# A fused attention and two-stage expert kernel: one normalization moved, two queues of small work re-placed, one output group reordered

## The chip, the cores and the metric
The kernel runs on one core of one Trainium2 chip. The metric is the device time of one execution in microseconds (us), as the median of several runs. One further execution was recorded by the hardware profiler, and all rows of the trace come from that one.

## What is computed
Three steps run one after the other; the second takes the first one's rows (2304 tokens of 512 values), the third takes the second one's.

```python
scores = scale * q @ k.T ; scores += min(-(cum_i - cum_j), 0)   # causal
attn = exp(scores - max); attn /= sum; x = attn @ v             # 4 x 8 heads, 576 x 64
...
e = argmax(x @ w_gate); gate_w = softmax(x @ w_gate)[e]         # 8 experts
x = gate_w * (relu(x @ w1[e]) @ w2[e])                          # 512 -> 1024 -> 512
...
xn = x / sqrt(mean(x*x) + 1e-6) * rms_g
out = (silu(xn @ w_gate2) * (xn @ w_val)) @ w_out               # 512 -> 1536 -> 512
```

## The kernel before, in words
All matrix products are in float32 split into two parts, high and low: a value is rounded by one engine (the high part, a cast) and the remainder is formed by another (the low part, a subtraction). A product is three matmuls, high by high, high by low and low by high.

**Attention** (to about 212 us of the trace) works on 16 pairs of heads. Its last part routes the tokens: `route` (L404 to L483) is a generator that computes the expert of each token, scatters the rows into one region of memory per expert with five indirect DMAs of GpSimd, and then calls `order_experts` (L486 to L537). That function sorts the experts by their count and writes the small table `nb`: where each expert's piece begins, who it is, and flags that are read at the very end. All of it is tiny VectorE instructions. A list `RANK` says how many steps of this generator are put behind each of the eight first products of expert 0.

**The experts** (`moe`, L857 to L952). Expert 0 is done first, in two portions: its first 256 rows ("early rows", in memory already), and 128 "late rows", which arrive with the last scatter and are loaded as `xl`. `gemm1` makes eight blocks of the hidden layer; each block ends with a Relu on ScalarE (L770) and a VectorE subtraction (L771). `gemm2` (L783) makes four column blocks. The late rows go through `rows_gemm1` (L821), are turned around by TensorE in `turn_tile` (L749, then the cast L751 on ScalarE and the subtraction L752 on VectorE), and go through `rows_gemm2` (L832). `finish` (L802) normalizes a portion's rows: a matmul that sums squares (L805), a square root on ScalarE (L807), a reciprocal (L808) and four multiplications (L811) on VectorE; `keep` (L795) sends the result to memory. `scaled_rows` and `turn_rows` (L849) do the same for the late rows. `x_transpose` (L738, L741, L742) prepares the rows of expert 1. In between, `split` takes the next piece of the experts' weights from its staging buffer, with a cast on ScalarE (L650) and a subtraction on GpSimd (L651), and then starts the load of another piece on SyncE's queue. Four staging buffers exist.

**The last stage** (`glu`, from about 460 us) has six groups of 384 tokens. Its first half (`glu_gemm1`, L1061) is one long run of matmuls. Its second half multiplies by the output weights: 72 steps n, each for one group g and one block f of twelve. A step's left operand was split six steps ahead by `glu_split` (cast L1076 on ScalarE, subtraction L1077 on GpSimd) and its nine matmuls are in `glu_gemm2` (L1086). Steps 0 to 23 alternate between the groups 0 and 1. The output weights arrive as 64-bit floats and are rebuilt by `decode`: bit operations and comparisons on VectorE (L1004, L1006, L1010, L1012, L1014), an absolute value on ScalarE (L1008), a rounding copy on VectorE (L1016, the cast) and a subtraction on GpSimd (L1017). Twelve such pieces are decoded ahead of the steps 1, 3, 5, 7, 9 and 11, two at each; four buffers hold them while they are rebuilt. At f = 11 a group's three tiles of outputs are copied by ScalarE (L1089) and scattered by an indirect DMA of GpSimd (L1090).

**The order of the work.** TensorE, ScalarE and VectorE run the instructions in the order of the program text; SyncE's queue too, inside `moe`. GpSimd's order, and SyncE's elsewhere, is chosen when the program is built, by data dependences. So an instruction that waits holds up all that is behind it on its engine.

Of the kernel before, what the change touches and what calls it, by code (L numbers as in the profile page):

```python
# [7 lines left out]
F32 = mybir.dt.float32  # L8
# [9 lines left out]
NTOK = B * S  # L18
# [4 lines left out]
NA = 256  # L23
# [618 lines left out]
def split(k, n=1, pool=None, bufs=0):  # L642
    nc = k.nc
    for _ in range(n):
        if k.staged:
            s, u, q, raw = k.staged.pop(0)
            if q == 0:
                new_unit(k, s, u)
            w = k.wt[s, u][:, q:q + 2]
            nc.scalar.copy(w[:, :, 0, :], raw)  # L650
            nc.gpsimd.tensor_tensor(w[:, :, 1, :], raw, w[:, :, 0, :].bitcast(F32), op=ALU.subtract)  # L651
            if pool or k.spool:
                feed(k, pool or k.spool, bufs or STG)
# [71 lines left out]
def x_transpose(k, s, kcs, tiles):  # L725
    if s not in k.xq:
        k.xq[s] = [k.rpool.tile([128, 4, CM], F32R, name=f"xt{n}{s}", tag=f"xt{n}", bufs=1) for n in range(2)]
    turn(k, k.x[s], tiles, k.xq[s], kcs)
# [16 lines left out]
def turn_tile(k, x, hi, lo):  # L745
    nc = k.nc
    ps = k.psum.tile([128, 512], F32, name=f"xq{k.uid()}", tag="b")
    for c in range(4):
        nc.tensor.transpose(ps[:, 128 * c:128 * c + 128], x[:, 128 * c:128 * c + 128], k.ident)  # L749
    p3 = ps.rearrange("p (c n) -> p c n", c=4)  # L750
    nc.scalar.copy(hi, p3)  # L751
    nc.vector.tensor_tensor(lo, p3, hi.bitcast(F32), op=ALU.subtract)  # L752
# [41 lines left out]
def keep(k, y, n, column):  # L794
    k.nc.sync.dma_start(out=k.ytd[:, :, bass.ds(column, n)], in_=y)  # L795


def column(k, piece):
    return number(k, OFF + piece, NTOK)


def finish(k, s, n):  # L802
    nc = k.nc
    ps = k.psum.tile([128, 512], F32, name=f"ms{s}", tag="b")
    nc.tensor.matmul(ps[:, 0:n], k.ones32, k.sq[s][:, 0:n], start=True, stop=True)  # L805
    r = k.sq[s][:, 0:n]
    nc.scalar.activation(r, ps[:, 0:n], AF.Sqrt, bias=k.eps6, scale=1.0 / DM)  # L807
    nc.vector.reciprocal(r, r)  # L808
    y = k.y[s][:, :, 0:n]
    for c in range(4):  # L810
        nc.vector.scalar_tensor_tensor(y[:, c, :], y[:, c, :], k.gv[:, c:c + 1], r, op0=ALU.mult, op1=ALU.mult)  # L811
    return y
# [44 lines left out]
def moe(k, close):  # L857
    k.y, k.sq = {}, {}

    def rank(n):  # L860
        for _ in range(n):
            next(k.last, None)

    spool, k.spool = k.spool, None
    feed(k, spool, STG, 2)
    k.order = [(s, u, q) for s in range(1, E) for u in range(4) for q in (0, 2)]
    row = ids(k, k.x[0], EARLY)
    keep_ids(k, row, 0)
    rank(RANK[0])
    for f in range(8):  # L870
        gemm1(k, 0, f, NA)
        rank(RANK[f + 1])
        if f == 3:
            load_late(k)
            load_x(k, 1)
            k.spool = spool
            feed(k, k.spool, STG, STG)
        if f < 2:
            split(k)
    first = tiles_of(CAP[0])  # L880
    gemm2(k, 0, 0, NA)
    gate(k, k.xl, ((0, 128),))
    gemm2(k, 0, 1, NA)
    xb = [k.rpool.tile([128, 4, CM], F32R, name=f"xb{n}", tag=f"xt{n}", bufs=1)[:, :, 0:128] for n in range(2)]
    turn_tile(k, k.xl[:, 0, :], *xb)
    row = ids(k, k.xl, ((0, 128),))
    keep_ids(k, row, column(k, 1))
    split(k)
    gemm2(k, 0, 2, NA)
    gate(k, k.x[1], first)  # L890
    split(k)
    gemm2(k, 0, 3, NA)
    split(k)
    k.hr = y_tile(k, "hr")[:, 0:1024]
    rows_gemm1(k, xb, 0)
    split(k)
    rows_gemm1(k, xb, 1)
    y = finish(k, 0, NA)
    hb = [k.mpool.tile([128, 8, CM], F32R, name=f"hb{n}", tag=f"h{n}")[:, :, 0:128] for n in range(2)]
    turn_tile(k, k.hr[:, 0:512], *[t[:, 0:4] for t in hb])  # L900
    x_transpose(k, 1, (0, 1), first)
    turn_tile(k, k.hr[:, 512:1024], *[t[:, 4:8] for t in hb])
    split(k)
    x_transpose(k, 1, (2, 3), first)
    row = ids(k, k.x[1], first)
    keep(k, y, NA, 0)
    yr = y_tile(k, "yr")[:, 0:1024].rearrange("p (a n) -> p a n", a=2)
    k.yr = yr[:, 0, :]
    rows_gemm2(k, hb)
    keep_ids(k, row, column(k, 2))  # L910
    split(k)
    for s in range(1, E):
        last = s == E - 1
        head = iter(())
        n = CAP[s - 1]
        if last:
            close()
            head = glu_head(k)
            next(head)
        else:  # L920
            load_x(k, s + 1)
        for f in range(8):
            gemm1(k, s, f, n)
            if s == 1 and f == 0:
                y = yr[:, 1, :].rearrange("p (c n) -> p c n", c=4)
                turn_rows(k, k.yr, y)
            if s > 1 and f == 1:
                y = finish(k, s - 1, CAP[s - 2])
            if f == 5:
                keep(k, y, CAP[s - 2] if s > 1 else LATE, column(k, s))  # L930
                if not last:
                    gate(k, k.x[s + 1], tiles_of(CAP[s]))
            if f % 2 or (s == 1 and f < 4):
                split(k)
            next(head, None)
        for c in range(4):
            gemm2(k, s, c, n)
            if not last:
                if c in (1, 2):
                    x_transpose(k, s + 1, (2 * c - 2, 2 * c - 1), tiles_of(CAP[s]))  # L940
                if c == 1:
                    row = ids(k, k.x[s + 1], tiles_of(CAP[s]))
                if c == 3:
                    keep_ids(k, row, column(k, s + 2))
            split(k)
            next(head, None)
    assert not k.staged and not k.order

    def tail():
        keep(k, finish(k, E - 1, CAP[-1]), CAP[-1], column(k, E))  # L950

    k.tail = tail  # L952


RANK = (9, 0, 17, 10, 0, 0, 0, 0, 0)


def glu_tiles(k, pool, tag, shape, n, dt=F32):
# [38 lines left out]
    nc.vector.tensor_tensor(high, high, low, op=ALU.bitwise_or)  # L997


def decode(k, loads):  # L1000
    nc = k.nc
    both = [(raw[:, :, 0], raw[:, :, 1], raw.bitcast(F32)[:, :, 1], w) for raw, w in loads]
    for low, high, hf, w in both:
        nc.vector.tensor_scalar(low, low, 29, None, op0=ALU.logical_shift_right)  # L1004
    for low, high, hf, w in both:
        nc.vector.scalar_tensor_tensor(low, high, 0xC0000000, low, op0=ALU.bitwise_and, op1=ALU.bitwise_or)  # L1006
    for low, high, hf, w in both:
        nc.scalar.activation(hf, hf, AF.Abs)  # L1008
    for low, high, hf, w in both:
        nc.vector.tensor_scalar(hf, hf, TINY, None, op0=ALU.max)  # L1010
    for low, high, hf, w in both:
        nc.vector.tensor_scalar(high, high, 3, 0x3FFFFFFF, op0=ALU.logical_shift_left, op1=ALU.bitwise_and)  # L1012
    for low, high, hf, w in both:
        nc.vector.tensor_tensor(high, high, low, op=ALU.bitwise_or)  # L1014
    for low, high, hf, w in both:
        nc.vector.tensor_copy(w[:, 0, :], hf)  # L1016
        nc.gpsimd.tensor_tensor(w[:, 1, :], hf, w[:, 0, :].bitcast(F32), op=ALU.subtract)  # L1017


# [57 lines left out]
    nc.gpsimd.tensor_tensor(c[:, 1, :], h, c[:, 0, :].bitcast(F32), op=ALU.subtract)  # L1077


def glu_gemm2(k, acc, n):  # L1080
    g, f = k.seq[n]
    w, c = k.wo[f], k.ring[n % 12]
    for t in range(3):
        cols = slice(128 * t, 128 * t + 128)
        for i, (a, b) in enumerate(((0, 0), (0, 1), (1, 0))):
            k.nc.tensor.matmul(acc[g][t], c[:, a, cols], w[:, b, :], start=f == 0 and i == 0, stop=f == 11 and i == 2)  # L1086
        if f == 11:
            o = new_raw(k).bitcast(F32).rearrange("p d two -> p (d two)")
            k.nc.scalar.copy(o, acc[g][t])  # L1089
            i = k.nc.gpsimd.indirect_dma_start(  # L1090
                out=k.out, out_offset=bass.IndirectOffsetOnAxis(ap=k.oid[:, g, t:t + 1], axis=0),
                in_=o, in_offset=None, bounds_check=NTOK - 1, oob_is_err=False,
            )
            of_rows(k, k.outs, i.ins, ())


def glu_head(k):
# [19 lines left out]
def glu(k):  # L1117
# [67 lines left out]
    for n, (g, f) in enumerate(k.seq):  # L1185
        if f == 0:
            acc[g] = [k.psum.tile([128, 512], F32, name=f"go{k.uid()}", tag="b") for _ in range(3)]
        if n < 24 and g == 1 and f + 6 < NF:
            decode(k, weights[0:2])
            weights = weights[2:]  # L1190
            if f + 8 < NF:
                weights += load_out(k, f + 8)
        if n + ahead < len(k.seq):
            glu_split(k, n + ahead)
        glu_gemm2(k, acc, n)
# [185 lines left out]
```

## Time and profile before

| what | value |
|---|---|
| median of 3 runs | 929.44 us (929.34 to 929.82) |
| the profiled execution, its own time | 934.07 us |
| its span, first to last instruction | 932.3 us |
| TensorE (matmuls) busy | 889.3 us, 95% |
| VectorE, ScalarE, GpSimd busy | 460.2, 410.8, 332.9 us |
| share of TensorE in the chain of work that ended last | 84% |
| share of VectorE in that chain | 6% |

The profiled execution took 4.6 us longer than the median, and its time holds 1.8 us outside the span. In a row of the timeline the first two numbers are the start and the length in us; xN counts merged instructions; what stands in brackets is the idle time of the engine just before and what ended it. In a row of windows each engine has its busy time and a count, then follow TensorE's granted clock (1.00 is full speed), the share of the DMA engines and the rate.

### The profile page before, as it was taken

To read this page: it belongs to the slowest core of one execution; us is meant where nothing else is said; L and a number is where in the kernel's file an instruction comes from. 1 tells how busy PE (TensorE), PEld (TensorE's weight loads), DVE (VectorE), ACT (ScalarE), POOL (GpSimd) and SP (SyncE) were. 2 spreads that over 40 slices of the span, in tenths; PEclk is the share of its full clock that TensorE was granted. 3 is DMA by queue.
4 is the path that set the end of the run, shared out by engine and by line. 5 is a ranking of instruction groups with operands and counts; after the bars stand their busy time and mean duration, and the time that the engine had idled before them with its cause. 6 is when DMAs were issued, how large, how long until landed. Compare 5 with 4: busy or idle time off the path is not lost.

```text
span 932.3 us, 15830 instructions
## 1 busy us (share of the span) xinstructions
PE 889.3 (95%) x5684; PEld 781.1 (84%) x5684; DVE 460.2 (49%) x1339; ACT 410.8 (44%) x1009; POOL 332.9 (36%) x320
## 2 busy tenths in 40 slices
PE   6999999998799999999899999999999998899995
PEld 3666666668699999999899999999999995588884
DVE  4555664637524354544685555444554699700000
ACT  5887887873655566665531111111111122333310
POOL 2001321034566667676111110011100146797541
PEclk9999999999999999999999999999999999999998
DMA  7996686323646566666531101111011122110001
GB/s 236 291 295 193 180 233 183 97 97 90 227 154 194 174 193 195 196 182 210 166 102 46 46 26 43 46 46 45 27 43 46 46 100 81 47 68 35 35 34 37
DMA packets 51388, 111.59 MB, mean 120 GB/s; under 512 B 6064, under 2 KB 14027, under 8 KB 51299
## 3 DMA queue, kind: packets, MB, share of 16 engines
q1 hardware_dynamic: 48339, 100.95, 35.7%
q0 software_dynamic: 2912, 9.46, 2.7%
q8 instruction: 47, 0.77, 0.3%
q14 instruction: 42, 0.34, 0.1%
q10 hardware_dynamic: 48, 0.07, 0.0%
HBM read 89.69 MB, written 20.76 MB: 118 GB/s over the span
## 4 chain that ended last, share of the span: by engine, by line
PE 84%; DVE 6%; issue 4%; POOL 3%; ACT 2%; DMA 1%; POOLq 0%; DVEq 0%; ACTq 0%
PE gg L1061 32%; PE g L783 11%; PE g L767 8%; PE go L1086 8%; PE t L306 6%; PE pvy L352 5%; PE s L261 5%; PE tl L380 3%; PE sm L274 2%; DVE raw L1014 1%; DVE raw L1004 1%; PE xp L738 1%; PE r L832 1%; POOL gx5b L1077 1%; PE r L821 1%
## 5 line engine op out<-in xcount | busy, mean ns | idle before, releaser
L1061 PE MATMUL gg<-gx,ws 128*128 128x384 f32 x1728 | 300.4, 335 | 0.0
L1061 PEld LDWEIGHTS gg<-gx,ws 128*128 128x128 f32 x1728 | 299.6, 188 | 0.1
L651 POOL TENSOR_TENSOR u<-raw,u 128x1024 fp32r<-128x1024 f32 x64 | 154.3, 2422 | 104.4 <-ACT u L650 100.4
L1017 POOL TENSOR_TENSOR ws<-raw,ws 128x256 fp32r<-128x256 f32 x48 | 36.7, 786 | 259.2 <-DVE ws L1016 259.2
L783 PE MATMUL g<-h,u 128*128 128x256 f32 (+7 forms) x768 | 109.0, 301 | 5.4 <-DVE h L771 4.2
L783 PEld LDWEIGHTS g<-h,u 128*128 128x128 f32 x768 | 104.5, 194 | 6.5 <-DVE h L771 4.6
L767 PE MATMUL g<-xt,u 128*128 128x256 f32 (+7 forms) x768 | 104.2, 295 | 0.0
L1067 ACT ACTIVATE gh<-gg 128x384 f32<-128x384 f32 x72 | 35.3, 491 | 152.9 <-PE gg L1061 152.9
L767 PEld LDWEIGHTS g<-xt,u 128*128 128x128 f32 x768 | 101.4, 188 | 0.8
L1008 ACT ACTIVATE raw<-raw 128x256 f32<-128x256 f32 x72 | 28.1, 442 | 124.9 <-DVE raw L1006 112.4
L287 ACT ACTIVATE p<-sc,nm 128x128 f32<-128x128 f32 (+3 forms) x128 | 72.4, 572 | 12.0 <-DVE nm L247 8.3
L1068 DVE TENSOR_TENSOR gh<-gg,gh 128x384 f32<-128x384 f32 x72 | 40.0, 555 | 74.8 <-ACT gh L1067 74.8
L247 DVE CUSTOM_DVE_ANT_0 sc<-s,in 128x128 f32<-128x128 f32 (+3 forms) x128 | 57.5, 489 | 39.0 <-PE s L264 19.9
L650 ACT CAST u<-raw 128x1024 fp32r<-128x1024 f32 x64 | 67.2, 1050 | 4.0 <-DMA raw<-in_w 4.0
L339 ACT COPY pt<-t 128x512 f32<-128x512 f32 (+3 forms) x160 | 62.2, 433 | 11.6 <-PE t L306 7.4
L306 PE MATMUL t<-ident,p 128*128 128x128 f32 x400 | 62.2, 281 | 1.6 <-ACT p L287 1.5
L1069 DVE TENSOR_TENSOR gh<-gg,gh 128x384 f32<-128x384 f32 x72 | 40.2, 558 | 44.8 <-PE gg L1061 41.6
L791 DVE TENSOR_TENSOR sq<-sq,sn 128x256 f32<-128x256 f32 (+7 forms) x24 | 15.7, 653 | 87.8 <-ACT sn L790 87.8
L352 PE MATMUL pvy<-pt,vp 128*64 128x512 f32 (+4 forms) x320 | 50.8, 433 | 1.5 <-ACT pt L339 0.8
L261 PE MATMUL s<-in 64*128 64x128 f32 (+3 forms) x256 | 51.5, 491 | 0.0
L306 PEld LDWEIGHTS t<-ident,p 128*128 128x128 f32 x400 | 43.8, 141 | 6.9 <-ACT p L287 2.2
L234 POOL COPY in<-in 64x64 f32<-64x64 f32 x32 | 8.0, 251 | 116.0 <-DMA in<-in_q 106.0
(232 smaller groups left out, 1207.4 us busy)
## 6 DMA issues: line engine op xcount, KB each, us to landing
raw<-in_w SPq DMA_DIRECT2D x64, 512.0 KB, 4.3
in<-cumd SPq DMA_DIRECT2D x30, 256.0 KB, 5.1
xs<-zrow SPq DMA_DIRECT2D x8, 771.0 KB, 10.2
raw<-in_wg SPq DMA_DIRECT2D x24, 256.0 KB
raw<-in_wv SPq DMA_DIRECT2D x24, 256.0 KB, 3.0
raw<-in_wo SPq DMA_DIRECT2D x24, 256.0 KB, 2.6
vp<-in_v SPq DMA_DIRECT2D x16, 320.0 KB, 5.9
in<-in_q SPq DMA_DIRECT2D x16, 288.0 KB, 5.3
```

The costliest lines, as they stand in the source:

```text
L247: k.nc.vector.tensor_tensor_reduce(out=out, in0=ps, in1=bias, scale=-0.125, scalar=3e38, op0=ALU.add, op1=ALU.min, accum_out=accum)
L261: nc.tensor.matmul(ps[h], st.q[r, 128 * i:128 * i + 128], st.k[r, 0:w], start=True, stop=False)
L287: k.nc.scalar.activation(out, st.s[i, h][:, 0:w], AF.Exp, bias=st.nm[:, n:n + 1], scale=-1.0, accum_out=acc)
L306: nc.tensor.transpose(ps[:, off:off + 128], src[:, 128 * j:128 * j + 128], k.ident)
L339: nc.scalar.copy(b, a)
L352: nc.tensor.matmul(st.y[r, a - 64:512], st.v[:, h, j, :], k.pt[:, h, o:o + S - a], start=j == 0, stop=j == 4)
L650: nc.scalar.copy(w[:, :, 0, :], raw)
L651: nc.gpsimd.tensor_tensor(w[:, :, 1, :], raw, w[:, :, 0, :].bitcast(F32), op=ALU.subtract)
L767: nc.tensor.matmul(ps[:, 0:n], w[:, f % 4, a, 128 * kc:128 * kc + 128], x[b][:, kc, 0:n], start=kc == 0 and i == 0, stop=kc == 3 and i == 2)
L783: nc.tensor.matmul(ps[:, 0:n], w[:, f % 4, a, 128 * c:128 * c + 128], k.h[b][:, f, 0:n], start=f == 0 and i == 0, stop=f == 7 and i == 2)
L1061: nc.tensor.matmul(ps, w[:, m, a, 128 * kc:128 * kc + 128], b[:, kc, :], start=kc == 0 and n == 0, stop=kc == 3 and n == 2)
L1086: k.nc.tensor.matmul(acc[g][t], c[:, a, cols], w[:, b, :], start=f == 0 and i == 0, stop=f == 11 and i == 2)
```

## The change
Four edits, none of which changes what is computed.

1. In `moe`, `finish(k, 0, NA)` moves behind both turned halves of the late rows, both transposes of expert 1 and one `split`; that `split` stays behind the transposes, which are no longer parted by it. The DMA `keep(k, y, NA, 0)` moves behind `rows_gemm2`. The late rows' result is written over `hr`, not into a new tile.
2. `RANK` spreads the end of the generator: three steps instead of ten behind the third product, then 1, 1, 1, 2, 2.
3. The rounding copy of the output weights, in the twelve pieces that are decoded between the steps, goes from VectorE to ScalarE.
4. In the last four steps (group 5, f from 8 to 11) the matmuls run tile by tile, each tile through its four blocks, so two tiles of outputs are complete before the third one's matmuls begin; the third tile's copy is shared by ScalarE and VectorE, half each.

```diff
@@ moe
     rows_gemm1(k, xb, 1)
-    y = finish(k, 0, NA)
     hb = [k.mpool.tile([128, 8, CM], F32R, name=f"hb{n}", tag=f"h{n}")[:, :, 0:128] for n in range(2)]
     turn_tile(k, k.hr[:, 0:512], *[t[:, 0:4] for t in hb])
     x_transpose(k, 1, (0, 1), first)
     turn_tile(k, k.hr[:, 512:1024], *[t[:, 4:8] for t in hb])
+    x_transpose(k, 1, (2, 3), first)
     split(k)
-    x_transpose(k, 1, (2, 3), first)
+    y = finish(k, 0, NA)
     row = ids(k, k.x[1], first)
-    keep(k, y, NA, 0)
-    yr = y_tile(k, "yr")[:, 0:1024].rearrange("p (a n) -> p a n", a=2)
+    yr = k.hr.rearrange("p (a n) -> p a n", a=2)
     k.yr = yr[:, 0, :]
     rows_gemm2(k, hb)
+    keep(k, y, NA, 0)
     keep_ids(k, row, column(k, 2))
...
-RANK = (9, 0, 17, 10, 0, 0, 0, 0, 0)
+RANK = (9, 0, 17, 3, 1, 1, 1, 2, 2)
@@ decode
-        nc.vector.tensor_copy(w[:, 0, :], hf)
+        (cast or nc.vector.tensor_copy)(w[:, 0, :], hf)
@@ glu_gemm2
+def glu_part(k, acc, n, t):
...
+        if g == NG - 1 and t == 2:
+            k.nc.scalar.copy(o[:, 0:256], acc[g][t][:, 0:256])
+            k.nc.vector.tensor_copy(o[:, 256:512], acc[g][t][:, 256:512])
+        else:
             k.nc.scalar.copy(o, acc[g][t])
...
+LASTF = 4
...
+    if n < len(k.seq) - LASTF:
+        for t in range(3):
+            glu_part(k, acc, n, t)
+    elif n == len(k.seq) - 1:
+        for t in range(3):
+            for m in range(LASTF):
+                glu_part(k, acc, n + 1 - LASTF + m, t)
@@ glu
-            decode(k, weights[0:2])
+            decode(k, weights[0:2], k.nc.scalar.copy)
```

## Rows read from the trace of the kernel before

**Rows 1.** Timeline of TensorE's matmuls, expert 0 and the late rows.
```profile
227.84 6.27 PE L783 MATMUL g<-h,u 128*128 128x256 f32 x38 [2.67 <-DVE h L771]
...
233.95 0.60 PE L749 MATMUL xq<-ident,xl 128*128 128x128 f32 x4
...
240.14 5.74 PE L821 MATMUL r<-u,xb 128*128 128x512 f32 x24
...
249.11 0.50 PE L832 MATMUL r<-u,hb 128*128 128x512 f32 x1
254.60 7.42 PE L832 MATMUL r<-u,hb 128*128 128x512 f32 x23 [4.99 <-DVE hb L752]
```

**Rows 2.** Timeline of VectorE, the same stretch.
```profile
224.72 0.15 DVE L516 CAST nb<-ogot 1x7 uint32<-1x7 f32 x1
...
226.91 1.73 DVE L771 SCALAR_TENSOR_TENSOR h<-g,h 128x256 fp32r<-128x256 f32 x5
...
248.34 1.75 DVE L808 RECIPROCAL sq<-sq 128x256 f32<-128x256 f32 x1 [3.00 <-ACT sq L807]
250.13 3.82 DVE L811 SCALAR_TENSOR_TENSOR y<-y,gv,sq 128x256 f32<-128x256 f32 x4
253.87 0.68 DVE L752 TENSOR_TENSOR hb<-xq,hb 128x512 fp32r<-128x512 f32 x1
```

**Rows 3.** Granted clock and busy time, four microseconds inside `rows_gemm2`.
```profile
254.00:258.00 4.00, 3.40 (x8) 2.72 (x9) 2.70 (x6) 0.00 (x0) 0.00 (x0) 0.50 0.79 250
```

**Rows 4.** Timeline of ScalarE, expert 0 and the late rows.
```profile
232.42 0.72 ACT L722 ACTIVATE xl<-xl 128x512 f32<-128x512 f32 x1 [0.56 <-DMA xl<-xs]
...
245.92 0.60 ACT L823 ACTIVATE hr<-r 128x512 f32<-128x512 f32 x1 [0.46 <-PE r L821]
246.53 1.28 ACT L807 ACT_TABLE_LOAD   x1
```

**Rows 5.** Line 811 over the whole trace: count, shortest, median and longest ns.
```profile
L811 DVE SCALAR_TENSOR_TENSOR y<-y,gv,sq x32: 471/520/2754, 250.1 to 466.8; 128x256 f32<-128x256 f32 x4, 128x312 f32<-128x312 f32 x4, 128x304 f32<-128x304 f32 x4, 128x300 f32<-128x300 f32 x4
```

**Rows 6.** Timeline of GpSimd, one weight subtraction in that stretch.
```profile
250.93 2.34 POOL L651 TENSOR_TENSOR u<-raw,u 128x1024 fp32r<-128x1024 f32 x1 [1.01 <-ACT u L650]
```

**Rows 7.** Timeline of VectorE, the decoding of output weights.
```profile
753.54 0.76 DVE L1014 TENSOR_TENSOR raw<-raw 128x256 uint32<-128x256 uint32 x2
...
777.06 2.38 DVE L1014 TENSOR_TENSOR raw<-raw 128x256 uint32<-128x256 uint32 x2
...
779.77 1.60 DVE L1004 TENSOR_SCALAR raw<-raw 128x256 uint32<-128x256 uint32 x2
...
785.52 0.49 DVE L1016 CAST gx2b<-raw 128x256 fp32r<-128x256 f32 x2
...
807.87 2.40 DVE L1014 TENSOR_TENSOR raw<-raw 128x256 uint32<-128x256 uint32 x2
```

**Rows 8.** Timeline of GpSimd, the same stretch.
```profile
776.88 2.28 POOL L1077 TENSOR_TENSOR gx5b<-gh,gx5b 128x384 fp32r<-128x384 f32 x2 [1.81 <-ACT gx5b L1076]
779.73 1.50 POOL L1017 TENSOR_TENSOR gx2b<-raw,gx2b 128x256 fp32r<-128x256 f32 x2 [0.57 <-DVE gx2b L1016]
```

**Rows 9.** Timeline of ScalarE, the same stretch.
```profile
781.79 0.78 ACT L1008 ACTIVATE raw<-raw 128x256 f32<-128x256 f32 x2 [4.58 <-DVE raw L1006]
```

**Rows 10.** Timeline of TensorE, its last wait in the output products.
```profile
808.87 1.88 PE L1086 MATMUL go<-gx3b,gx4b 128*128 128x512 f32 x7 [0.48 <-POOL gx4b L1077]
```

**Rows 11.** DMA issues by tile: count, size, median us from issue to landing.
```profile
raw<-in_wo SPq DMA_DIRECT2D x24, 256.0 KB, 2.6
```

**Rows 12.** Timeline of ScalarE, the last outputs.
```profile
920.55 0.59 ACT L1089 COPY raw<-go 128x512 f32<-128x512 f32 x1 [20.17 <-PE go L1086]
921.29 1.29 ACT L1089 COPY raw<-go 128x512 f32<-128x512 f32 x2 [0.16 <-PE go L1086]
```

**Rows 13.** Timeline of GpSimd, the last outputs.
```profile
921.41 0.99 POOL L1090 DMA_INDIRECT out<-raw,oid  x1 [15.18 <-ACT raw L1089]
...
923.99 0.98 POOL L1090 DMA_INDIRECT out<-raw,oid  x1 [0.30 <-issue]
```

More of the change, by code (lines that the diff above doesn't have):

```diff
@@ L997, in as_f32, with decode @@
     nc.vector.tensor_tensor(high, high, low, op=ALU.bitwise_or)
-def decode(k, loads):
+def decode(k, loads, cast=None):
     nc = k.nc
@@ L1077, in glu_split, with glu_gemm2 @@
     nc.gpsimd.tensor_tensor(c[:, 1, :], h, c[:, 0, :].bitcast(F32), op=ALU.subtract)
-def glu_gemm2(k, acc, n):
+def glu_part(k, acc, n, t):
     g, f = k.seq[n]
     w, c = k.wo[f], k.ring[n % 12]
[L1083 to L1088, printed above, removed]
-            k.nc.scalar.copy(o, acc[g][t])
[L1090 to L1094, printed above, removed]
+    cols = slice(128 * t, 128 * t + 128)
+    for i, (a, b) in enumerate(((0, 0), (0, 1), (1, 0))):
+        k.nc.tensor.matmul(acc[g][t], c[:, a, cols], w[:, b, :], start=f == 0 and i == 0, stop=f == 11 and i == 2)
+    if f == 11:
+        o = new_raw(k).bitcast(F32).rearrange("p d two -> p (d two)")
+        if g == NG - 1 and t == 2:
+            k.nc.scalar.copy(o[:, 0:256], acc[g][t][:, 0:256])
+            k.nc.vector.tensor_copy(o[:, 256:512], acc[g][t][:, 256:512])
+        else:
+            k.nc.scalar.copy(o, acc[g][t])
+        i = k.nc.gpsimd.indirect_dma_start(
+            out=k.out, out_offset=bass.IndirectOffsetOnAxis(ap=k.oid[:, g, t:t + 1], axis=0),
+            in_=o, in_offset=None, bounds_check=NTOK - 1, oob_is_err=False,
+        )
+        of_rows(k, k.outs, i.ins, ())
+LASTF = 4
+def glu_gemm2(k, acc, n):
+    if n < len(k.seq) - LASTF:
[5 more added lines that the diff above has]
+                glu_part(k, acc, n + 1 - LASTF + m, t)
 def glu_head(k):
```

## The prediction, made before the changed kernel ran

> **What bounds the kernel now.** I read the page first: TensorE is busy for almost the whole span and holds most of the chain of waits, so time can only come from TensorE's gaps and its slow stretches. Then the timeline of TensorE, looking in brackets for what ended each gap, and the other engines' timelines at those places. Four places touch the change.
>
> *Expert 0's second product.* TensorE has started `gemm2` and then stands 2.67 us [rows 1] for a low part of the hidden layer: VectorE makes the last five only after the whole expert ordering, from 226.91 us [rows 2].
>
> *The late rows.* The first matmul of `rows_gemm2` runs at 249.11 us; then TensorE stands 4.99 us for `hb` [rows 1]. VectorE was busy with the early rows' normalization, a reciprocal of 1.75 and multiplications of 3.82, and made the first `hb` at 253.87 [rows 2]. After the gap the clock is at half speed, 0.50, the 1.2 GHz level [rows 3]: 23 matmuls take 7.42 us where 24 of the same width in `rows_gemm1` took 5.74 [rows 1].
>
> *The output weights.* Six decodings, from 777.06 to 807.87 us, follow each other in a loop of (807.87 - 777.06) / 5 = 6.16 us [rows 7]. The two steps that each feeds need 18 matmuls; nine of this width take about 2.1 us (the 7 at 808.87 take 1.88 [rows 10]), so TensorE needs some 4.1 us of a loop and waits the rest. Its last such wait ends at 808.87, on GpSimd's low part [rows 10].
>
> *The end.* The third copy of outputs ends at 921.29 + 1.29 = 922.58 [rows 12]; its indirect DMA begins at 923.99 because GpSimd is still issuing the one before [rows 13].
>
> **The change part by part.** The sums are made in the profiled execution, 934.07 us, which is 4.6 us or 0.5% above the median of 929.44; I subtract the same gain from the median.
>
> *Ordering spread.* Nothing is added or removed; the same VectorE instructions stand elsewhere. The fourth low part can now start at about 224.8, behind the step that writes `nb` at 224.72 [rows 2], the last ones around 227.6 to 228.4, each one delayed by the small steps still ahead of it. So the column block ends some 2 us earlier at best. But the next thing on TensorE, the turn of the late rows at 233.95 [rows 1], needs rows that land and are scaled until 232.42 + 0.72 = 233.14 [rows 4]. That load waits for the scatters, which the change leaves alone. What is late next is thus the late rows, and the gain is 233.95 - 233.2 = **0.75 us**; the bounds are 0, if the clock falls all the same and stays low longer, and 0.8. I take 0.75, as either clock reaches 233.2. ScalarE keeps up: it stood 0.46 us before the late Relu [rows 4], and TensorE's second turn needs that Relu only after the first turn and a transpose.
>
> *Normalization behind the splits.* The four turned blocks go first on VectorE. Their subtractions read PSUM and need about 0.68 each [rows 2], ScalarE's casts about as much as the Relu of the same size, 0.60 [rows 4]. So both `hb` are there when TensorE, which has the same transposes to do as now, comes to `rows_gemm2` where its first matmul already stands: 249.11 [rows 1]. It then ends at 249.11 + 5.74 = 254.85 in place of 254.60 + 7.42 = 262.02: **7.17 us**, of it 4.99 the gap and 2.2 the slow clock. The cost is hidden: the square root comes behind the five casts, the split and the table load of 1.28 [rows 4], at about 251; reciprocal 1.75 [rows 2]; four multiplications at the median of 0.52 [rows 5], to about 254.8. The late rows need VectorE's next reciprocal at about 255 (matmuls to 254.1 with the lead of 0.75, then two ScalarE passes). The cover is thin. If it fails, TensorE waits at the transposes of `yr`. In `keep` one DMA moves on SyncE's queue; behind it stand the ids and the next weight load, and that load waits anyway for a buffer that the next split frees, so nothing is late. The tile saved costs nothing. Bounds: 4.99 (the clock stays low) to 7.9.
>
> *Casts on ScalarE.* Per decoding VectorE loses two copies of together 0.49 [rows 7]; ScalarE gains two, which I price like its Abs passes on the same buffers, 0.78 for two [rows 9]. But more moves than that. On ScalarE the splits of the left operands now stand behind these casts, which wait for L1014. So GpSimd's four subtractions come in one run, weights first. Now the L1014 pair takes 2.38 while GpSimd subtracts (776.88 to 779.16 [rows 8]) and 0.76 when alone [rows 7]; L1004 likewise shares 1.60 with GpSimd's 1.50 [rows 7, 8]. In the rows a VectorE instruction and a GpSimd one alternate, at 0.75 per pair for the weights (1.50 / 2) and 1.14 for the splits (2.28 / 2). The new loop, from the start of L1014: 0.4 for its first half, 0.4 cast, 0.15 handover; then 1.50 + 2.28 of GpSimd with L1004, L1006 and half of L1010 between; then some 0.7 of L1010 and L1012, an estimate as two fifths of the loop's rest (6.16 - 2.38 - 0.49 - 1.60 = 1.7). Sum 5.4 us, over five loops 5 x 0.73 = 3.6 saved. Against it, the operand that TensorE waits for last: now it comes 808.87 - 807.87 = 1.0 after L1014 began [rows 7, 10], then 0.95 + 1.50 + 1.0 = 3.4 after: 2.4 lost. Net **1.2 us** gained. Bounds: below, the case of full blocking (a rival); above, a loop of 4.7, at which the reload of a buffer (2.6 [rows 11], after 0.95 + 1.50) becomes the bound: 5 x 1.46 - 2.4 = 4.9.
>
> The Trainium skill (SBUF — State Buffer, "Who interferes with whom") says that a VectorE instruction with two SBUF inputs and a GpSimd one that reads SBUF exclude each other for the whole instruction, and that the loser blocks fully. The long rows of L1014 bear that out; the weights' pairs, 0.75, look more like overlap. By the rule alone this part would lose time instead.
>
> *The end.* The third tile's copy is halved, about 0.4 us between 0.3 (half of 0.59) and 0.59 [rows 12], and its DMA finds GpSimd free. From a copy's end to its DMA it is 921.41 - (920.55 + 0.59) = 0.27 [rows 12, 13]. So it begins at 922.58 - 0.59 + 0.4 + 0.27 = 922.66, not 923.99: **1.3 us**, bounds 1.1 and 1.45. The second tile is done twelve matmuls earlier, over 2 us, and its DMA takes 0.99. The matmuls are the same number.
>
> Sum: 0.75 + 7.17 + 1.2 + 1.3 = 10.4, and 929.44 - 10.4 = **919.0 us**. In the page's slices TensorE is full through the other experts, and each weight load hangs on the split before it, so the lead should carry through the experts.
>
> **The rivals.**
> *Full blocking.* Every VectorE instruction of a decoding and every GpSimd subtraction exclude each other. Then the loop is their sum: on VectorE, without waits, some 2.9 (0.76, then an estimate of 0.65 for L1004 by its width, then 1.7 less ScalarE's part), on GpSimd 1.50 and 2.28 less what these rows hold of waiting, some 3.5; about 6.4: 5 x 0.24 lost, and 2.4, so the part costs 3.6. Total gain 5.6: **923.8**. For it: L811 took up to 2754 ns [rows 5] beside a subtraction of 2.34 [rows 6]. Against: the 0.75 pairs. Chance 0.2.
> *The early rows meet a GpSimd split.* The moved split's subtraction (2.34 [rows 6]) starts at about 250 and should end near 252.3, before the multiplications; if it comes later, one of them waits as now, the late rows' reciprocal with it, and TensorE stands some 1.8 us: **920.8**. Chance 0.15.
> *Reload-bound loop, the good end.* Loop 4.7: **915.3**. Chance 0.1.
> *Slower than before: one piece in flight.* If GpSimd takes the operands' subtractions first, as it does now, the weight buffers come free late: 0.4 + 0.78 + 0.4 + 2.28 + 1.50, reload 2.6, L1004 with 0.65, the rest 1.7, about 10.3 per loop. If the next pieces are not already loaded, that whole chain is the loop: 5 x 4.1 + 2.4 lost against 9.2 gained elsewhere, **943**. It turns the sign from a loop of 7.5 us. Against: four buffers hold two decodings, which halves it. Chance 0.02.
> *The lead is given back* before the last stage, by weights that come late: only the last two parts stay, **927**. SyncE's loads were never what TensorE waited for. Chance 0.03.
>
> **How the numbers follow.** The forecast has a chance of 0.5. Its own bounds and the three rivals beside it span 914.5 to 925.0, which leaves out the last two rivals and some tails, also that the profiled execution is not quite the median one. About 0.2% of the time, 2 us, is what a measurement can tell from no change. Faster 0.95, same 0.02, slower 0.03.
>
> **What would show it.** Right: no gap ahead of `rows_gemm2`, 24 matmuls in 5.7 us at full clock, `rows_gemm2` ending about 8 us earlier; the turn of the late rows 0.7 us earlier with a wait for `xl`; loops of 5.4 us, and the last wait of the output products about 1 us nearer to the preceding stage; a last DMA 0.3 us behind its copy. Wrong: a new gap at the transposes of `yr`, loops of 6.2 us or more, or a TensorE gap among the experts where none was.

## The result, and the profile after

| | before | changed | |
|---|---|---|---|
| median | 929.62 us (929.34 to 929.82, 4 runs) | 921.36 us (920.23 to 922.34, 4 runs) | ratio 0.9911, 95% interval 0.9894 to 0.9928 |
| profiled execution | 934.07 us | 922.34 us | |
| its span | 932.3 us | 920.6 us | |

The median fell by 8.3 us; the forecast was 10.4 (919.0 us). The two profiled executions differ by more, 11.6 us of span, and the table says where. Each stretch is cut at rows that both traces have.

| stretch | before | changed | difference |
|---|---|---|---|
| start to the routing's first matmul (L443) | 215.03 | 211.64 | -3.4 |
| from there to the turn of the late rows (L749, `xl`) | 18.92 | 18.43 | -0.5 |
| from there to the end of `rows_gemm2` (L832) | 28.07 | 21.11 | -7.0 |
| from there to the first matmul of the last stage (L1061) | 198.51 | 199.66 | +1.15 |
| from there to the first output product | 300.43 | 300.41 | 0.0 |
| from there to the end of TensorE's last wait | 47.91 | 46.46 | -1.45 |
| from there to the last matmul's end | 113.04 | 113.11 | +0.1 |
| from there to the last DMA's start (GpSimd) | 2.08 | 1.24 | -0.8 |
| from there to the end of the span | 8.28 | 8.57 | +0.3 |

The first row is not the change's: attention is the same in both. Among the experiments below, which leave it alone too, that matmul starts at 214.3 to 215.8 us in the four kernels that ran on one chip, and at 210.7 to 213.1 in the six that ran on another; the kernel before took 934.0 us on the first and 929.3 to 929.4 on the second. The profiled 934.07 fits the first chip and not the second, so the chip is the likely cause of this row; no trace of one kernel on both chips shows it. Without the row 8.2 us remain, as in the medians.

TensorE's timeline after the change. The number behind PE is the line, which past L1080 is a few lines off: L1085 is what L1086 was.
```profile
211.64 0.19 PE L443 MATMUL rk<-oh,tri 128*128 128x40 bf16 x1
...
223.42 0.62 PE L783 MATMUL g<-h,u 128*128 128x256 f32 x3 [0.94 <-DVE h L771]
224.66 5.58 PE L783 MATMUL g<-h,u 128*128 128x256 f32 x32 [0.61 <-DVE h L771]
230.07 0.60 PE L749 MATMUL xq<-ident,xl 128*128 128x128 f32 x4
...
245.34 5.84 PE L832 MATMUL r<-u,hb 128*128 128x512 f32 x24
...
253.26 0.66 PE L849 MATMUL yt<-ident,hr 128*128 128x128 f32 x4 [0.37 <-ACT hr L842]
...
438.13 12.87 PE L783 MATMUL g<-h,u 128*128 128x248 f32 x86 [1.50 <-DVE h L771]
...
797.71 1.90 PE L1085 MATMUL go<-gx3b,gx4b 128*128 128x512 f32 x7 [0.49 <-POOL gx4b L1077]
```
The 4.99 us ahead of `rows_gemm2` [rows 1] are gone, and its 24 matmuls run in one block of 5.84. The wait of 2.67 [rows 1] became two of 0.94 and 0.61. No wait for `xl` is shown ahead of the turn. The last wait of the output products is still one for GpSimd's low part.

VectorE's timeline after the change, at the same places.
```profile
221.41 0.40 DVE L771 SCALAR_TENSOR_TENSOR h<-g,h 128x256 fp32r<-128x256 f32 x1
...
243.15 0.69 DVE L752 TENSOR_TENSOR hb<-xq,hb 128x512 fp32r<-128x512 f32 x1 [2.67 <-ACT hb L751]
...
247.91 1.75 DVE L808 RECIPROCAL sq<-sq 128x256 f32<-128x256 f32 x1 [1.91 <-ACT sq L807]
249.70 1.67 DVE L811 SCALAR_TENSOR_TENSOR y<-y,gv,sq 128x256 f32<-128x256 f32 x4
252.32 0.16 DVE L841 RECIPROCAL ss<-ss 128x1 f32<-128x1 f32 x1 [0.95 <-ACT ss L840]
...
766.39 0.63 DVE L1010 TENSOR_SCALAR raw<-raw 128x256 f32<-128x256 f32 x2 [0.22 <-ACT raw L1008]
766.94 0.49 DVE L1012 TENSOR_SCALAR raw<-raw 128x256 uint32<-128x256 uint32 x2
767.35 0.75 DVE L1014 TENSOR_TENSOR raw<-raw 128x256 uint32<-128x256 uint32 x2
...
784.59 0.75 DVE L1006 SCALAR_TENSOR_TENSOR raw<-raw 128x256 uint32<-128x256 uint32 x2
785.93 1.88 DVE L1010 TENSOR_SCALAR raw<-raw 128x256 f32<-128x256 f32 x2 [0.59 <-ACT raw L1008]
787.74 1.30 DVE L1012 TENSOR_SCALAR raw<-raw 128x256 uint32<-128x256 uint32 x2
...
794.26 0.75 DVE L1014 TENSOR_TENSOR raw<-raw 128x256 uint32<-128x256 uint32 x2
...
911.36 0.42 DVE L1090 COPY raw<-go 128x256 f32<-128x256 f32 x1 [116.35 <-ACT raw L1089]
```
The first `hb` is made at 243.15, released by ScalarE's cast, 6.6 us ahead of the multiplications; before, it stood behind them [rows 2]. The four multiplications take 1.67 in place of 3.82 [rows 2], and VectorE idles 0.95 us before the late rows' reciprocal: the cover held. L1014 takes 0.75 in each of the six decodings of the loop, from 767.35 to 794.26, not 2.38 [rows 7].

ScalarE's and then GpSimd's timeline after the change.
```profile
229.08 0.73 ACT L722 ACTIVATE xl<-xl 128x512 f32<-128x512 f32 x1 [2.44 <-DMA xl<-xs]
...
910.90 0.37 ACT L1089 COPY raw<-go 128x256 f32<-128x256 f32 x1 [2.20 <-PE go L1085]
```
```profile
246.16 2.43 POOL L651 TENSOR_TENSOR u<-raw,u 128x1024 fp32r<-128x1024 f32 x1 [1.06 <-ACT u L650]
...
784.47 2.18 POOL L1017 TENSOR_TENSOR gx3b<-raw,gx3b 128x256 fp32r<-128x256 f32 x2 [1.44 <-ACT gx3b L1016]
786.62 2.06 POOL L1077 TENSOR_TENSOR gx1b<-gh,gx1b 128x384 fp32r<-128x384 f32 x2
...
912.06 0.97 POOL L1093 DMA_INDIRECT out<-raw,oid  x1 [2.11 <-DVE raw L1090]
```
ScalarE now stands 2.44 us for the late rows where it stood 0.56 [rows 4]. The rows did not come earlier: they are scaled 18.17 us after the routing's first matmul (229.08 + 0.73 - 211.64), and were at 18.11 before [rows 4]. The turn follows 0.26 us later. The subtraction of the moved split ends at 246.16 + 2.43 = 248.59, 1.1 us ahead of the multiplications. At the very end VectorE's half of the last copy starts behind ScalarE's half, not beside it.

### The profile page after: what moved, and what is told of

It is laid out like the page before. It is cut to its first block, busy times and chain, and to the rows that moved or that the text cites. A ratio compares the mean times of both kernels' runs of the same rounds, so it can differ in the third digit from the quotient of the medians.

```text
span 920.6 us, 15813 instructions
## 1 busy us (share of the span) xinstructions
PE 889.1 (97%) x5684; PEld 782.9 (85%) x5684; DVE 452.0 (49%) x1328; ACT 416.5 (45%) x1021; POOL 333.1 (36%) x320
## 4 chain that ended last, share of the span: by engine, by line
PE 87%; DVE 7%; ACT 2%; POOL 1%; issue 1%; DMA 1%; POOLq 0%; DVEq 0%; ACTq 0%
PE gg L1061 30%; PE go L1085 12%; PE g L783 11%; PE g L767 9%; PE t L306 6%; PE s L261 5%; PE pvy L352 5%; PE tl L380 3%; PE sm L274 2%; DVE raw L1010 1%; PE xp L738 1%; DVE raw L1006 1%; DVE raw L1014 1%; DVE raw L1004 1%; ACT raw L1008 1%
## 5 line engine op out<-in xcount | busy, mean ns | idle before, releaser
L1061 PE MATMUL gg<-gx,ws 128*128 128x384 f32 x1728 | 300.4, 335 | 0.0
L1061 PEld LDWEIGHTS gg<-gx,ws 128*128 128x128 f32 x1728 | 299.6, 188 | 0.1
```

The lines of the kernel that those rows point to most:

```text
L1061: nc.tensor.matmul(ps, w[:, m, a, 128 * kc:128 * kc + 128], b[:, kc, :], start=kc == 0 and n == 0, stop=kc == 3 and n == 2)
```

## The experiments

**Each part alone.** Four kernels, each the kernel before with one part of the change, beside the kernel before on one chip (934.0 us there). The other experiments ran on a second chip, where the kernel before takes 929.3 to 929.4 us; four of them were timed in one run each, and for those the trace is the evidence, not the time.

*The normalization alone* (`finish`, the transposes, the split, `keep` and the tile as in the change).

> The kernel before with the moved normalization alone. My theory (order on VectorE): the 4.99 us gap and the slow clock after it both go, rows_gemm2 has no gap, its 24 matmuls take 5.7 to 5.9 us, and the time falls by 7 us (6 to 8), ratio 0.9925. Rival one (the parts need each other: without the lead of the ordering the late Relu comes too late): a gap of 0.5 us or more stays ahead of rows_gemm2. Rival two (the lead is lost again at the experts' last product): below 3 us of gain.

926.7 us, ratio 0.9923 (0.9906 to 0.9939): 7.3 us. TensorE's timeline of this kernel:
```profile
249.12 5.84 PE L832 MATMUL r<-u,hb 128*128 128x512 f32 x24
...
257.05 0.66 PE L849 MATMUL yt<-ident,hr 128*128 128x128 f32 x4 [0.37 <-ACT hr L842]
```
No gap; `rows_gemm2` starts at 249.12, where its first matmul already stood before, at 249.11 [rows 1]. From the turn of the late rows to its end it takes 21.11 us, as in the whole change. So this part needs no other, and both rivals fall.

*The ordering alone* (`RANK` as in the change).

> The kernel before with the spread ordering alone. My theory: the turn of the late rows moves only to where their load allows, 0.4 to 0.8 us earlier; since the gap ahead of rows_gemm2 is set by VectorE's normalization behind ScalarE's Relu, at most 0.8 us come out at the end, ratio 0.999 to 1.000. Rival (the wait of 2.67 us is worth itself and its slow clock): 2 us or more earlier at the turn and at the end, ratio 0.998 or lower.

934.05 us, ratio 1.0 (0.999 to 1.0009). TensorE's timeline of this kernel:
```profile
227.58 0.62 PE L783 MATMUL g<-h,u 128*128 128x256 f32 x3 [0.95 <-DVE h L771]
228.81 5.58 PE L783 MATMUL g<-h,u 128*128 128x256 f32 x32 [0.61 <-DVE h L771]
234.22 0.60 PE L749 MATMUL xq<-ident,xl 128*128 128x128 f32 x4
```
The waits are those of the whole change, the turn comes 18.43 us after the routing's first matmul. But `d_last_only`, which leaves the ordering as it was, has 18.46 in its trace. So even the half microsecond of the table is within what that stretch varies by. And the gap of 4.99 us ahead of `rows_gemm2` stays: from the turn to its end it takes 28.78 us, against 28.07 before, and nothing of the half microsecond is left there. The rival of 2 us falls.

*The casts alone* (`decode` with ScalarE's copy).

> The kernel before with the output weights' casts on ScalarE alone. My theory: the loop of one decoding falls from 6.16 to about 5.4 us, the operands come 2.4 us later after the last L1014, and 1.0 to 1.6 us come out. Rival one (VectorE and GpSimd exclude each other fully): loop 6.2 us or more, and the time rises by 2 us or more. Rival two (the gain in the changed kernel was a matter of phase): no change within 0.3 us from the first decoding to TensorE's last wait.

933.23 us, ratio 0.999 (0.998 to 0.9999). VectorE's first and last L1014 of the five loops, and TensorE's last wait:
```profile
776.52 0.75 DVE L1014 TENSOR_TENSOR raw<-raw 128x256 uint32<-128x256 uint32 x2
...
803.47 0.75 DVE L1014 TENSOR_TENSOR raw<-raw 128x256 uint32<-128x256 uint32 x2
```
```profile
806.90 1.89 PE L1086 MATMUL go<-gx3b,gx4b 128*128 128x512 f32 x7 [0.48 <-POOL gx4b L1077]
```
The loop is (803.47 - 776.52) / 5 = 5.39 us, and the last wait ends 806.90 - 803.47 = 3.43 after the last L1014. From the first output product to there it takes 46.45 us, 1.45 less than before, the same as in the whole change. Both rivals fall. The time alone, 0.8 us with an interval that almost reaches 1, would not have shown it.

*The last steps alone.*

> The kernel before with the last steps tile by tile alone. My theory after the changed kernel's trace: VectorE's half of the last copy begins only after ScalarE's half, so the last DMA starts some 0.7 us behind the copy's begin plus its handover, and 0.8 us (0.6 to 0.9) come out between the last matmul's end and the last DMA's start. Rival (the halves run side by side, and the changed kernel's trace was an accident): 1.3 us.

933.4 us, ratio 0.9997 (0.9988 to 1.0007), too small to be timed. VectorE's half of the last copy, and GpSimd's last DMA:
```profile
922.21 0.42 DVE L1090 COPY raw<-go 128x256 f32<-128x256 f32 x1 [111.01 <-ACT raw L1089]
```
```profile
922.91 0.97 POOL L1093 DMA_INDIRECT out<-raw,oid  x1 [2.10 <-DVE raw L1090]
```
The DMA starts 1.24 us after the last matmul's end, 0.83 less than before; again VectorE waited for ScalarE, and the rival of 1.3 us falls.

**Order or the wait for GpSimd?** In the kernel before, one split moves and nothing else.
```diff
-    split(k)
     x_transpose(k, 1, (2, 3), first)
+    split(k)
```

> The kernel before, in which only one weight split moves behind the second transpose of expert 1; the normalization stays ahead. It parts the order of VectorE's work from the wait for GpSimd: one multiplication took 2.6 us in place of 0.5 because the split's subtraction ran beside it. My theory (order first, the wait for GpSimd second): the four multiplications take 1.7 to 2.5 us, the gap ahead of rows_gemm2 shrinks from 4.99 to about 3 us and stays. Rival (the gap is the wait for GpSimd, and the moved split in the change did the work): the gap falls below 1 us.

926.55 us in one run, beside 929.32. VectorE, TensorE and GpSimd:
```profile
245.63 1.67 DVE L811 SCALAR_TENSOR_TENSOR y<-y,gv,sq 128x256 f32<-128x256 f32 x4
```
```profile
247.96 6.96 PE L832 MATMUL r<-u,hb 128*128 128x512 f32 x23 [2.84 <-DVE hb L752]
```
```profile
247.08 2.48 POOL L651 TENSOR_TENSOR u<-raw,u 128x1024 fp32r<-128x1024 f32 x1 [1.66 <-ACT u L650]
```
The subtraction now starts when the last of the multiplications is nearly done (247.08 against 245.63 + 1.67 = 247.30). They take 1.67 in place of 3.82, and the gap shrinks by as much, 2.15, from 4.99 to 2.84. So the gap had two causes: 2.15 us was VectorE standing for GpSimd, 2.84 the order of its own work. The matmuls behind the shorter gap are still slow, 6.96.

**What the ordering is bounded by.** The changed kernel, with `RANK = (9, 0, 17, 3, 0, 0, 0, 0, 5)`.

> The changed kernel, with the last two steps of the expert ordering put behind the eighth product, so that no small VectorE work stands between the hidden layer's low parts. My theory (the late rows' load is the next bound): the two waits of 0.9 and 0.6 us in expert 0's second product go, the wait for the late rows grows by as much, and from the routing's first matmul to the turn of the late rows it takes 18.4 us as in the changed kernel (within 0.2). Rival (VectorE still sets the turn): 17.5 us or less.

922.84 us in one run. TensorE's timeline, then its windows:
```profile
219.51 6.19 PE L783 MATMUL g<-h,u 128*128 128x256 f32 x48
229.22 1.12 PE L749 MATMUL xq<-ident,xl 128*128 128x128 f32 x4 [3.52 <-ACT xl L722]
...
230.20 7.98 PE L783 MATMUL g<-h,u 128*128 128x256 f32 x48
```
```profile
226.00:230.00 4.00, 0.78 (x4) 0.79 (x5) 0.26 (x1) 1.27 (x3) 0.00 (x0) 0.75 0.64 176
230.00:234.00 4.00, 4.00 (x21) 3.91 (x20) 0.86 (x2) 1.69 (x3) 0.00 (x0) 0.50 0.99 327
```
The same two windows of the changed kernel, and its 48 matmuls behind the turn:
```profile
226.00:230.00 4.00, 4.00 (x24) 4.00 (x24) 0.00 (x0) 1.37 (x3) 0.00 (x0) 0.62 0.55 121
230.00:234.00 4.00, 4.00 (x36) 3.98 (x36) 1.12 (x2) 1.95 (x5) 0.00 (x0) 1.00 1.02 363
```
```profile
230.53 5.89 PE L783 MATMUL g<-h,u 128*128 128x256 f32 x48
```
As expected the two waits are gone, and the turn still comes 18.50 us after the routing's first matmul: the load sets it. So this run, and not the changed kernel's own trace, shows the load as the bound. What was not expected: the wait for `xl` is 3.52 us, more than the two waits that went. With the change the slow clock (0.62) falls on the work ahead of the late rows, which has time to spare, and it is full behind; here the work behind the wait runs at 0.50, the next 48 matmuls take 7.98 us where they took 5.89, and from the turn to the end of `rows_gemm2` it takes 23.72 in place of 21.11. Here the removal of small waits cost 2.6 us (one trace of this kernel; the four other variants of the changed kernel, which leave this place alone, have 21.11 to 21.16).

**The last copy.** The changed kernel without the halving.
```diff
-        if g == NG - 1 and t == 2:
...
+        k.nc.scalar.copy(o, acc[g][t])
```

> The changed kernel, with the third tile of the last outputs copied by ScalarE alone. My theory: the two halves run one after the other, so the halving costs time; the last DMA starts 0.2 to 0.4 us earlier against the last matmul's end than in the changed kernel (0.85 to 1.05 us behind it in place of 1.24). Rival (the halves overlap or the copy is not what the DMA waits for): the same or later.

920.19 us in one run. ScalarE's last copy and GpSimd's last DMA:
```profile
908.95 0.59 ACT L1088 COPY raw<-go 128x512 f32<-128x512 f32 x1 [2.20 <-PE go L1085]
```
```profile
909.81 0.97 POOL L1089 DMA_INDIRECT out<-raw,oid  x1 [1.81 <-ACT raw L1088]
```
The DMA starts 0.94 us after the last matmul's end, 0.30 earlier than with two halves. One copy of 0.59 beats 0.37 and 0.42 in a row.

**The operand's split first.** The changed kernel, with `glu_split` ahead of `decode` in each step.
```diff
+        if n + ahead < len(k.seq):
+            glu_split(k, n + ahead)
         if n < 24 and g == 1 and f + 6 < NF:
...
-        if n + ahead < len(k.seq):
-            glu_split(k, n + ahead)
```

> The changed kernel, with the split of a left operand put ahead of the decoding in the program, at each step. My theory: what TensorE waits for last is the operand whose cast stands behind the last decoding's casts on ScalarE; with it ahead, TensorE's last wait ends 1 to 2.5 us earlier, counted from the first of the output products, where the loop of a decoding stays at 5.2 to 5.6 us. Rival one (the loop of VectorE and GpSimd alone sets the end, whatever the order on ScalarE): within 0.3 us. Rival two (the operands' subtractions again run beside L1014, as before the change): the loop goes back to 6 us and the end with it.

920.79 us in one run. TensorE's last wait:
```profile
798.02 8.07 PE L1085 MATMUL go<-gx3b,gx5b 128*128 128x512 f32 x34 [0.47 <-POOL gx5b L1077]
```
As it was put, the expectation missed: this wait ends 47.14 us after the first output product, 0.7 later than the 46.46 of the changed kernel. But it stands ahead of a later step, nine matmuls on (the 165th, not the 156th), so the two ends don't compare. From the first output product to the last matmul's end, which does, it takes 158.2 us in place of 159.6: 1.4 us, as much as was expected of the wait. That the order on ScalarE is what gave it is argued from the edit. L1014 begins at 767.78 and 794.59 at the two ends, a loop of 5.36. Rival two falls with the loop, rival one with the 1.4 us.

**Where the lead shrank.** The changed kernel, with the last stage's first weights decoded later in `glu_head`.
```diff
-    yield
-    yield
-    decode(k, weights[0:2])
-    yield
-    decode(k, weights[2:4])
-    yield
-    for n in (0, 0, 0, 0, 1, 2, 3, 4):
+    for _ in range(6):
+        yield
+    decode(k, weights[0:2])
+    yield
+    yield
+    decode(k, weights[2:4])
+    yield
+    for n in (1, 2, 3, 4):
```

> The changed kernel, with the decoding of the last stage's first weights put behind the last expert's hidden layer (four to five steps later). The lead won at the late rows was carried through the experts in full and shrank by 1.1 us at the last expert's second product, where TensorE stands 2.8 us for VectorE in both kernels and the clock was slow for longer in the changed one. My theory (that loss is the clock after this same wait, no cost of the change): without the wait the clock stays at full speed there, and from the end of rows_gemm2 to the first matmul of the last stage it takes 195 us or less in place of 198.5 and 199.7; 3 to 5 us come out, ratio 0.986 against the kernel before. Rival (the late stages are held by loads that do not move): 198 us or more, and no gain.

916.01 us, ratio 0.9857 (0.9841 to 0.9874). That is 5.4 us below the changed kernel's median, somewhat over the 3 to 5 expected. Windows at the last expert's second product, first of the kernel before, then of the changed one; the number behind the five engines is TensorE's granted clock:
```profile
448.96:452.96 4.00, 4.00 (x22) 4.00 (x23) 2.10 (x5) 1.31 (x3) 0.96 (x2) 0.60 0.66 192
452.96:456.96 4.00, 4.00 (x35) 4.00 (x35) 1.72 (x3) 1.42 (x4) 0.00 (x0) 0.97 0.34 83
```
```profile
438.13:442.13 4.00, 4.00 (x19) 4.00 (x19) 2.10 (x5) 0.62 (x3) 0.93 (x2) 0.50 0.66 183
442.13:446.13 4.00, 4.00 (x28) 4.00 (x28) 0.96 (x1) 1.34 (x5) 0.00 (x0) 0.75 0.18 31
```
TensorE's timeline of `head_later`, the same product:
```profile
433.24 11.30 PE L783 MATMUL g<-h,u 128*128 128x248 f32 x96
```
In both kernels TensorE stands twice there, 1.3 us for ScalarE's Relu and 1.5 for VectorE's low part (the expectation put all 2.8 down to VectorE). Behind the second wait the clock was back at full speed earlier before the change, and the same 86 matmuls took 11.74 there and 12.87 after. They also vary among kernels that have no edit near them; here they are in the kernel before and in `a_order_only`, where the clock behind the wait was 1.00:
```profile
448.96 11.74 PE L783 MATMUL g<-h,u 128*128 128x248 f32 x86 [1.50 <-DVE h L771]
```
```profile
449.94 10.15 PE L783 MATMUL g<-h,u 128*128 128x248 f32 x86 [1.50 <-DVE h L771]
```
Without the waits 96 matmuls take 11.30, and the stretch falls to 193.74 us. In kernels that have the waits and no edit near them, the stretch took from 196.92 (`a_order_only`) to 199.72 (`c_split_first`). All of that spread is in this one product: from the end of `rows_gemm2` to its first matmul every trace of this study takes 182.6 us. `d_one_copy`, which differs from the changed kernel in the last copy alone, has 198.46. So the 1.15 us of the table is this spread, no cost of the change.

**All three together**: the later decoding, the split first and the single copy, on the changed kernel.

> The changed kernel with what three experiments pointed to, together: the later decoding at the last expert, the operand's split ahead of the decoding, one copy for the last tile. My theory (three separate places, each on TensorE's path): 5.0 + 1.4 + 0.3 us less than the changed kernel, about 914.5 us and a ratio of 0.984 against the kernel before (0.982 to 0.986). Rival (the clock gives part of it back in the output products, where the waits are now fewer but no shorter): 916 us, a ratio of 0.9855 or higher.

915.18 us (914.05 to 916.48), ratio 0.9844 (0.983 to 0.9858), the lowest median of this study; the runs of `head_later` lie inside its spread. In its trace the three places show 193.72, 158.0 and 0.94 us, as each alone; my 914.5 us lies inside the spread of the runs, the rival's 0.9855 inside the interval too, though the stretches speak for the first.

## Why the prediction was right, and what was off

Of the 10.4 us forecast 8.3 came, and 921.36 us lies inside the stated 914.5 to 925.0.

**The normalization** was the term that carried it: 7.17 forecast, 6.96 in the trace, 7.3 timed alone. The reading that `rows_gemm2` would start where its first matmul stood came out to 0.01 us, and the thin cover held with 0.95 us to spare. What the prediction did not part is that 2.15 of the gap was VectorE standing for GpSimd; it didn't need to, as the move takes both away. The rival of the early rows meeting a split stayed out by 1.1 us.

**The casts**: 1.2 forecast, 1.45 in the trace. Loop 5.4 forecast, 5.38 measured ((794.26 - 767.35) / 5), operand after L1014 3.4 forecast, 3.45 measured. The start of GpSimd's run, 0.95 us into the loop, was right too, but the 5.4 is in part luck: the run of four subtractions was priced at 3.78 and took 3.79 to 4.22, and the rest of the loop, priced at 0.7, took 0.27 to 0.68. The rival of full blocking is wrong for this loop: it needed 6.4. The good end, 4.7, and the loop of one piece in flight, 7.5 or more, did not come either. The Trainium skill (SBUF — State Buffer, "Who interferes with whom") has the two engines exclude each other for a whole instruction where VectorE's has two SBUF inputs or runs in a two-port mode. Single rows bear that out, the multiplications that took 3.82 and then 1.67. But from 784.47 to 789.04, which is 4.57 us, both did work that alone takes 5.4: GpSimd about 1.5 and 2.0, VectorE 0.75, 0.63 and 0.49. So a sum of both engines' times was an upper bound. One pair out of that stretch shows how both can be true:
```profile
785.93 0.88 DVE L1010 TENSOR_SCALAR raw<-raw 128x256 f32<-128x256 f32 x1 [0.59 <-ACT raw L1008]
785.92 0.74 POOL L1017 TENSOR_TENSOR gx3b<-raw,gx3b 128x256 fp32r<-128x256 f32 x1
```
VectorE's instruction, 0.30 alone, took 0.88 and ended some 0.15 us behind GpSimd's, so it was held; GpSimd's took its usual 0.74. One waits, but the pair costs little more than the longer of the two.

**The end**: 1.3 forecast, 0.83 measured. The step that failed is "the third tile's copy is halved, about 0.4 us". I priced two halves side by side; they ran one after the other, 0.37 and 0.42, which costs more than one copy of 0.59. Both halves read one bank of PSUM. The Trainium skill (PSUM — Partial Sum Buffer, "PSUM bank collisions raise a hardware error") says that two engines must not touch the same bank and quadrant at once, reads included; that the trace shows VectorE released by ScalarE agrees. But both halves also write one tile, `raw`, and no run here parts the two causes. A look at that page would have told me to price the halves one after the other.

**The ordering**: 0.75 forecast, at most 0.5 in the trace and nothing in the time. The place of the bound was right, the late rows' load, as `a_after_f7` shows; the sign named for it, a wait for `xl`, is not in the changed kernel's trace, where matmuls at a clock of 0.62 filled the time until the rows came. Its size was within the spread of the stretch, which I had not asked for.

**The lead through the experts** was carried in full, up to the last expert: 182.6 us from the end of `rows_gemm2` to its second product, before and after. The 1.15 us behind that are the clock after two waits that both kernels have, and the profiled executions differ in it as two kernels with the same code there do. The prediction spoke of weights that might come late, and the equal stretches show none that did.

By the stretches of the two traces: 10.4, less 0.25 (ordering), 0.2 (normalization), 0.5 (end), 1.15 (clock) and 0.4 of the last rows of the table, plus 0.25 (casts), is 8.2. This is one execution of each kernel. That the medians differ by as much may be chance in part, as the clock's 1.15 us need not be in every execution.

## What to carry to other kernels

In an engine that runs its instructions in order, look at what stands in front of the instruction that another engine waits for. Here moving it away closed a gap of 4.99 us, and the move was priced well by where the waiter's first instruction already stood. Before comparing two traces, cut them at rows that both have: here 3.4 us of the difference lay in work that the change doesn't touch, and 1.15 in the clock behind waits that both kernels have. Two engines that were to copy halves of one output tile side by side did it one after the other, and one copy was faster; price such a split that way until a trace shows otherwise.

## What was not expected of the hardware

One wait of 3.52 us left TensorE at half its clock, 1.2 GHz, for what came behind it, and cost 2.6 us by the end of `rows_gemm2`. With waits of 0.94 and 0.61 in the work ahead, the clock fell too, but early, and was full again when the late rows came. So small waits ahead of a wait that stays are not always worth removing: in this pair of kernels the slow clock moved to where it counted. And behind the same two waits of 1.3 and 1.5 us at the last expert the same 86 matmuls took from 10.15 us, at full clock, to 12.95 (`c_split_first`); what decides that between executions stays open.
